# The second layer's product with w1 and w2 in seven half-block products over pairs of 384 tokens

## The chip, the cores and the metric

The kernel runs on one core of a Trainium2 chip. The metric is device time in microseconds (us) from the start to the end of the one launch. TensorE (PE) multiplies, with weight loads (PEld) that overlap; VectorE (DVE), ScalarE (ACT) and GpSimd (POOL) work element by element; SyncE (SP) issues most DMAs. Every engine takes its own instructions in the order in which the kernel wrote them.

## What is computed

Windowed attention over q, k, v (4 batches, 8 heads, 576 positions, 64 wide) gives x of 2304 tokens by 512. Then come two layers, both in float32:

```python
h = x @ w_in                         # 512 -> 2048
x2 = (h * (1.0 / (1.0 + np.exp(-h)))) @ w_out   # 2048 -> 512
a = x2 @ w1                          # 512 -> 1024
b = x2 @ w2                          # 512 -> 1024
out = ((a * b) @ w3) @ w_out2        # 1024 -> 1024 -> 512
```

## The kernel before

A float32 operand is kept as two fp32r parts, high and low (`split`: an ACT copy makes the high part, a DVE subtraction the low one). A product is the sum of three matmuls: high by high, low by high, high by low. The matrices arrive as 64-bit words, a piece being 128 by 512; class `Convert` turns each into its two parts in small steps ("micros"): a load into one of four `raw` buffers, `rebias` (L386, ACT), two `bits` operations (L394 and L396, DVE), `high` (L405, ACT) and `low` (L411, DVE). Letters in the strings `START`, `SLOT` and `GROUP` say where a micro ("m") stands between the parts of the matrix work; so the order of every engine is written by hand.

The first layer runs over five chunks of tokens (`CH1`) and 16 blocks `f` of w_in and w_out: `h_part` (L524), `g_ops`, `g_split`, `x2_part` (L552). Attention is woven into its first chunks. In the last chunk the buffers `wf` of w_in and w_out come free one after the other, and the pieces of w1, w2, w3 and w_out2 are converted into them. x2 is stored to DRAM (`x2d`) chunk by chunk.

The second layer first makes W' = w3 @ w_out2 in two halves (`wp_group`, L503, 96 matmuls each, with the conversion of w3 beside them). Then it runs over five chunks of tokens (`CH2`: four of 512, one of 256) and eight blocks `j` of 128 columns of w1 and w2. For each (chunk, j), `ab_part` (L600) makes a and b, 12 matmuls each: four blocks of the 512 inputs by three products of parts. `p_ops` copies a (L610, ACT) and multiplies by b (L611, DVE); `p_split` splits the product into `pg` (L454, ACT, L455, DVE); `o_part` (L630) multiplies by W' into one PSUM bank for each 128 tokens. a and b have two PSUM banks each. The order is: a and b of the next j, then the output of this j, so that each product has a whole j's time to be split.

## Time and profile before

| what | us |
|---|---|
| median of 3 runs (849.88 to 852.16) | 850.1 |
| the profiled execution | 851.98 |
| its span, first to last instruction | 850.0 |
| PE busy in that span | 829.0 |
| DVE busy | 400.2 |
| ACT busy | 361.1 |
| POOL busy | 56.7 |

The page gives the busy time of each engine, and in 40 slices of 21.25 us where it lies. The chain of waits says which engine's work ended last at each step. The views by line and form give the mean duration of one instruction of each shape; the timeline gives start and duration in order of time, with runs of the same line merged (x12 is twelve instructions); the windows view sums busy time in a stretch.

### The profile page before, as it was taken

The page shows a single profiled execution, that of the slowest core. Times are in us where ns is not written, and L with a number is a line of the kernel's source. Part 1 is how long each engine was busy: PE and PEld are TensorE (multiplying, and loading weights), DVE is VectorE, ACT ScalarE, POOL GpSimd, SP SyncE. Part 2 cuts the span into 40 slices and gives each one's busy share as a digit, 9 for nine tenths or more (in the row PEclk, how much of TensorE's full clock was granted, in tenths as well). Part 3 has the DMA queues.
Part 4 walks back from the last instruction along what each step waited for, and adds up shares of the span by engine and source line. Part 5 has one row for each costly group of instructions (what it writes and reads, how often), then busy time and mean ns, then how long its engine had stood idle before and what let it go on. Part 6 is the DMA issues. An engine that isn't in the chain of part 4 may idle for free.

```text
span 850.0 us, 11943 instructions
## 1 busy us (share of the span) xinstructions
PE 829.0 (98%) x4312; PEld 684.3 (81%) x4312; DVE 400.2 (47%) x1097; ACT 361.1 (42%) x950; POOL 56.7 (7%) x70
## 2 busy tenths in 40 slices
PE   5799999999999999999999999999999999999998
PEld 3467777788788999888888888888888888888897
DVE  4968888455534663222375656683122122112121
ACT  5857777565534763322354543462122122112121
POOL 4311110011100220000000000000000000000000
PEclk9999999999999999999999999999999999999999
DMA  5655555221101311200063326460030030020010
GB/s 166 201 175 180 185 183 172 74 63 50 49 27 41 94 26 49 76 0 1 14 210 124 99 100 222 133 190 1 1 99 1 1 99 1 1 75 0 1 51 26
DMA packets 42635, 69.20 MB, mean 81 GB/s; under 512 B 5328, under 2 KB 25040, under 8 KB 42576
## 3 DMA queue, kind: packets, MB, share of 16 engines
q1 hardware_dynamic: 42208, 68.09, 25.6%
q8 instruction: 34, 0.56, 0.3%
q10 hardware_dynamic: 368, 0.35, 0.2%
q14 instruction: 25, 0.20, 0.1%
HBM read 58.98 MB, written 9.44 MB: 80 GB/s over the span
## 4 chain that ended last, share of the span: by engine, by line
PE 95%; DMA 2%; DVE 2%; SPq 0%; ACT 0%; issue 0%; POOL 0%; POOLq 0%
PE x L552 24%; PE h L524 24%; PE ab L600 23%; PE o L630 12%; PE wp L503 5%; PE o L256 2%; PE s L185 2%; PE s L190 2%; PE t L238 2%; DMA raw_i<-in_w_in_dram 1%; DMA kz<-in_kT_dram 1%; DVE sm L206 1%; DVE at L245 0%; SPq L162 0%; DVE xT L267 0%
## 5 line engine op out<-in xcount | busy, mean ns | idle before, releaser
L552 PE MATMUL x<-g,wf 128*128 128x512 f32 (+1 forms) x960 | 217.7, 371 | 0.0
L524 PE MATMUL h<-xT,wf 128*128 128x512 f32 (+1 forms) x960 | 217.2, 373 | 0.0
L600 PE MATMUL ab<-xT,wf 128*128 128x512 f32 (+1 forms) x960 | 203.7, 368 | 0.0
L600 PEld LDWEIGHTS ab<-xT,wf 128*128 128x128 f32 x960 | 168.2, 188 | 30.6
L524 PEld LDWEIGHTS h<-xT,wf 128*128 128x128 f32 x960 | 167.5, 190 | 29.7
L552 PEld LDWEIGHTS x<-g,wf 128*128 128x128 f32 x960 | 166.2, 188 | 30.9
L611 DVE TENSOR_TENSOR pa<-pa,ab 128x512 f32<-128x512 f32 (+1 forms) x40 | 25.4, 635 | 189.3 <-PE ab L600 188.4
L535 DVE SCALAR_TENSOR_TENSOR t<-t,h 128x512 f32<-128x512 f32 (+1 forms) x80 | 50.6, 632 | 129.2 <-ACT t L534 129.1
L630 PE MATMUL o<-wf,pg 128*128 128x512 f32 x432 | 104.3, 390 | 0.0
L630 PEld LDWEIGHTS o<-wf,pg 128*128 128x128 f32 x432 | 80.6, 188 | 16.4
L534 ACT ACTIVATE t<-h 128x512 f32<-128x512 f32 (+1 forms) x80 | 44.1, 551 | 104.9 <-PE h L524 102.7
L218 ACT ACTIVATE sm<-sm,nm 96x128 f32<-96x128 f32 x192 | 74.5, 390 | 11.3 <-DVE nm L206 11.3
L610 ACT ACTIVATE pa<-ab 128x512 f32<-128x512 f32 (+1 forms) x40 | 22.2, 555 | 119.1 <-PE ab L600 119.1
L230 POOL TENSOR_TENSOR sm<-sm,rs 96x512 f32<-96x512 f32 x48 | 51.9, 1081 | 263.6 <-DVE rs L228 130.0
L455 DVE TENSOR_TENSOR g<-t,g 128x512 fp32r<-128x512 f32 (+1 forms) x80 | 54.4, 680 | 31.8 <-ACT g L454 30.7
L454 ACT ACTIVATE pg<-pa 128x512 fp32r<-128x512 f32 (+1 forms) x40 | 23.6, 589 | 104.2 <-DVE pa L611 104.2
L454 ACT ACTIVATE g<-t 128x512 fp32r<-128x512 f32 (+1 forms) x80 | 46.8, 586 | 30.0 <-DVE t L535 29.7
L206 DVE CUSTOM_DVE_ANT_0 sm<-s,mask 96x128 f32<-96x128 f32 x192 | 43.8, 280 | 8.4 <-POOL ident masks.py:199 4.3
L503 PE MATMUL wp<-wf,xT 128*128 128x512 f32 x192 | 43.9, 389 | 0.0
L503 PEld LDWEIGHTS wp<-wf,xT 128*128 128x128 f32 x192 | 36.0, 188 | 7.5
L190 PE MATMUL s<-kz,q 128*96 128x256 f32 x112 | 31.3, 409 | 7.4 <-DMA kz<-in_kT_dram 7.4
L455 DVE TENSOR_TENSOR pg<-pa,pg 128x512 fp32r<-128x512 f32 (+1 forms) x40 | 25.6, 639 | 26.3 <-ACT pg L454 26.3
(63 smaller groups left out, 595.4 us busy)
## 6 DMA issues: line engine op xcount, KB each, us to landing
raw_i<-in_w_in_dram SPq DMA_DIRECT2D x16, 512.0 KB, 4.3
raw_u<-in_w_out_dram SPq DMA_DIRECT2D x16, 512.0 KB, 5.7
raw<-in_w_dram SPq DMA_DIRECT2D x16, 512.0 KB, 3.3
raw_w<-in_w_dram SPq DMA_DIRECT2D x16, 512.0 KB, 4.4
v<-in_v_dram SPq DMA_DIRECT2D x96, 64.0 KB, 2.5
kz<-in_kT_dram SPq DMA_DIRECT2D x95, 56.0 KB, 2.5
q<-in_qT_dram SPq DMA_DIRECT2D x15, 288.0 KB, 2.9
x2d<-x2s SPq DMA_DIRECT2D x8, 512.0 KB, 3.3
```

The costliest lines, as they stand in the source:

```text
L190: nc.tensor.matmul(s_ps[:QB, c], t[:, QB * i:QB * i + QB], kz[n % 3][:, :, k0:k0 + P], start=True, stop=True,)
L206: nc.vector.tensor_tensor_reduce(sm[:, c, h], s_ps[:QB, c, h], mask[:, mo + c], -SCALE, 3.0e38, ALU.add, ALU.min, nm[:, 2 * c + h:2 * c + ...
L218: nc.scalar.activation(sm[:, c, h], sm[:, c, h], AF.Exp, bias=nm[:, j:j + 1], scale=-1.0, accum_out=su[:, j:j + 1],)
L230: nc.gpsimd.tensor_tensor(f, f, rs.to_broadcast([QB, 4, P]), op=ALU.mult)
L454: nc.scalar.activation(dst[:, 0], src, AF.Copy)
L455: nc.vector.tensor_sub(dst[:, 1], src, f32(dst[:, 0]))
L503: nc.tensor.matmul(wp_ps[i], a[:, i // 2, sa, i % 2 * P:(i % 2 + 1) * P], o[:, sb], start=(jt == 0 and x == 0), stop=(jt == NG - 1 and x = ...
L524: nc.tensor.matmul(ps, win(f, sa, kt), xT[:, kt, sb, r0:r0 + n], start=(kt == 0 and x == 0), stop=(kt == KT - 1 and x == 2),)
L535: nc.vector.scalar_tensor_tensor(t, t, 1.0, ps, op0=ALU.add, op1=ALU.mult)
L552: nc.tensor.matmul(xps[c][m][:, :n], wout(f, sa, m), g[:, sb], start=(f == 0 and sa == 0 and sb == 0), stop=(f == NF - 1 and sb == 1),)
L600: nc.tensor.matmul(ps[:, :n], w12(j, x, sa, kt), xT[:, kt, sb, r:r + n], start=(kt == 0 and y == 0), stop=(kt == KT - 1 and y == 2),)
L630: nc.tensor.matmul(ops[c][m], g[:, sa, m * P:(m + 1) * P], wp_v(j, sb), start=(j == 0 and sa == 0 and sb == 0), stop=(j == NG - 1 and sa = ...
```

## The change

a and b are made by Strassen's scheme in Winograd's form. Weights and x2 are cut in half along the 512 inputs; the 1024 columns of w1 are paired as block j with block j + 4 and those of w2 likewise; tokens are paired as two blocks of 384 (`T2`), so 2304 tokens are three pairs (`NPR`). A "set" is one of w1, w2 with one j of 0 to 3: eight sets. Each set and pair takes seven products (`PROD`) of half blocks, 6 matmuls each (two input blocks by three products of parts) with 384 columns, where the same piece of work had eight such products.

The weight operand of a product is a half block or a sum of half blocks: `Jobs.combine` makes the four sums of a set (on DVE for sets 0 to 2, on POOL for sets 3 to 7), and `high` and `low` split seven units of 256 columns per set instead of the four that the two pieces hold. The token operands are likewise half blocks or sums (`x_sum`, `x_split`), seven per pair. `collect` adds up the seven products from two PSUM banks: the first is copied to s1 by ACT, the others are added by DVE, seven additions per set. When w2's set of a j has been added too, the four blocks of a * b are multiplied (on POOL in the first pair, on DVE in the others), copied by ACT and split by DVE. `o_group` is three matmuls of the output; twelve of them per two sets stand one behind each product.

Four sets fit in SBUF. All eight are stored to DRAM (`set_io`) as they are made, and in the second and third pair four of them are loaded back; the order of the sets turns round in every other pair. The first two sets' products stand between the parts of W''s second half. W''s first half uses the PSUM banks that attention had, and its first group stands inside the last block of the first layer.

```diff
 CH1 = [(0, 512), (512, 512), (1024, 256), (1280, 512), (1792, 512)]
-CH2 = [(0, 512), (512, 512), (1024, 512), (1536, 512), (2048, 256)]
-R2 = [0, 512, 0, 512, 1024]
+T2 = 384
+NPR = NT // (2 * T2)
+NSET = NG
...
-    "hmmHmxXmmtgmm",
+    "hmHmxtgmmmmXmmmm",
 )
-LAST_SLOT = "ahxXHtg"
-GROUP = "mmmmmmmmmmmmmmmwmmmmmmW"
+GROUP = ("mmmmw", "mmmmW")
+MICROS = 2
...
+    setd = [dram.tile([P, 7, 512], F32, tag=f"set{i}", name=f"setd_{i}") for i in range(NSET)]
...
+    def set_io(s, store):
+        for part, n in ((0, 4), (1, 3)):
+            t = f32(wf[2 * (s % 4) + part][:, :512 * n])
+            d = setd[s].rearrange("p u k -> p (u k)")[:, 2048 * part:2048 * part + 512 * n]
+            nc.sync.dma_start(out=d, in_=t) if store else nc.sync.dma_start(out=t, in_=d)
...
+        def combine(self, k, x):
+            a, b = self.yf(k, 0), self.yf(k, 1)
+            if x == 0:
+                self.sum[k] = tmp1.tile([P, 4, 256], F32, tag="ss", name=f"ss_{k}")
+            t = self.sum[k]
+            eng = nc.gpsimd if self.jobs[k][1] > 2 else nc.vector
+            if x == 0:
+                eng.tensor_add(t[:, 0], b[:, :256], b[:, 256:])
+            elif x == 1:
+                eng.tensor_sub(t[:, 1], t[:, 0], a[:, :256])
+            elif x == 2:
+                eng.tensor_sub(t[:, 2], a[:, :256], b[:, :256])
+            else:
+                eng.tensor_sub(t[:, 3], a[:, 256:], t[:, 1])
...
+        def low(self, k, i):
+            dst, y = self.parts(k)[i]
+            nc.vector.tensor_sub(dst[:, 1], y, f32(dst[:, 0]))
+            srcs, d = self.jobs[k]
+            if len(srcs) == 2 and i == 2:
+                set_io(d, True)
...
     def wp_group(k, part):
         half, jt = divmod(k, NG)
         if jt == 0 and part == 0:
-            wp_ps[:] = [ps_x.tile([P, 512], F32, tag="x", name=f"wp_{half}_{i}") for i in range(4)]
+            wp_ps[:] = []
+        if jt == 0:
+            for i in range(2 * part, 2 * part + 2):
+                pool, tag = (ps_x, "x") if half else (ps_h, "h") if part else (ps_a, "a")
+                wp_ps.append(pool.tile([P, 512], F32, tag=tag, name=f"wp_{half}_{i}"))
...
+    PROD = [("11", "11"), ("S2", "T2"), ("12", "21"), ("S3", "T3"), ("S1", "T1"), ("22", "T4"), ("S4", "22")]
...
+    def g_block(j, i, s):
+        b = 4 * (j % 2) + i
+        o = 1024 * (b % 2) + T2 * s
+        return wf[8 + b // 2][:, o:o + T2]
...
+    def order(pr):
+        return [0, 1, 2, 3, 4, 5, 6, 7] if pr % 2 == 0 else [6, 7, 4, 5, 2, 3, 0, 1]
...
+    def product(s, i):
+        if not banks:
+            banks[:] = [ps_h.tile([P, 512], F32, tag="h", name=f"bank{k}") for k in range(2)]
+        b = banks[count[0] % 2][:, :T2]
+        count[0] += 1
+        a, x = PROD[i]
+        n = 0
+        for kt in range(2):
+            for sa, sb in ((0, 0), (1, 0), (0, 1)):
                 nc.tensor.matmul(
-                    ps[:, :n], w12(j, x, sa, kt), xT[:, kt, sb, r:r + n],
-                    start=(kt == 0 and y == 0), stop=(kt == KT - 1 and y == 2),
-                )
-        ab[c, j, x] = ps
-    def p_ops(c, j):
-        n = CH2[c][1]
-        a, b = ab.pop((c, j, 0)), ab.pop((c, j, 1))
-        t = gp.tile([P, 512], F32, tag="t", name=f"pa_{c}_{j}", bufs=1)[:, :n]
-        nc.scalar.activation(t, a[:, :n], AF.Copy)
-        nc.vector.tensor_mul(t, t, b[:, :n])
-        pt[c, j] = t
-    def p_split(c, j):
-        n = CH2[c][1]
-        g = gp.tile([P, 2, 512], F32R, tag="g", name=f"pg_{c}_{j}")[:, :, :n]
-        split(g, pt[c, j])
-        pt[c, j] = g
-    def o_part(c, j):
-        t0, n = CH2[c]
-        nm = n // P
-        if j == 0:
-            ops[c] = [ps_x.tile([P, 512], F32, tag="x", name=f"o_{c}_{m}") for m in range(nm)]
-        g = pt.pop((c, j))
-        todo = [(m, 0, sb) for m in range(nm) for sb in (0, 1)] + [(m, 1, 0) for m in range(nm)]
-        if j == NG - 1:
-            todo.sort(key=lambda z: z[0])
-        for m, sa, sb in todo:
+                    b, a_op(s, a, sa, kt), b_op(x, sb, kt),
+                    start=(n == 0), stop=(n == 5),
+                )
+                n += 1
+        return b
...
+    def collect(pr, s, i, b, j):
+        if not cst:
+            for k in ("s1", "u2", "u3", "c11", "c22", "c21", "c12"):
+                cst[k] = fin.tile([P, T2], F32, tag=k, name=k)
+        c = cst
+        s1, u2, u3 = c["s1"], c["u2"], c["u3"]
+        second = s % 2
+        now = [op for at, op in behind if at <= count[0]]
+        behind[:] = [z for z in behind if z[0] > count[0]]
+        if i == 0:
+            nc.scalar.activation(s1, b, AF.Copy)
+        elif i == 1:
+            nc.vector.tensor_add(u2, s1, b)
+        elif i == 3:
+            nc.vector.tensor_add(u3, u2, b)
+        else:
+            k, u, t = {2: ("c11", s1, s1), 4: ("c22", u3, s1), 5: ("c21", u3, u3), 6: ("c12", u2, u2)}[i]
+            nc.vector.tensor_add(t if second else c[k], u, b)
+            if i == 4:
+                nc.vector.tensor_add(u2, u2, b)
+        for op in now:
+            op()
+        if i in (2, 4, 5, 6):
+            if second:
+                n = ("c11", "c22", "c21", "c12").index(k)
+                hi, lo = (g_block(j, n, x) for x in range(2))
+                (nc.gpsimd if pr == 0 else nc.vector).tensor_mul(c[k], c[k], t)
+                nc.scalar.activation(hi, c[k], AF.Copy)
+                behind.append((
+                    count[0] + (2 if pr == 0 else 1), lambda: nc.vector.tensor_sub(lo, c[k], f32(hi))
+                ))
...
+    def o_group(pr, jj, n, m):
+        j = order(pr)[2 * jj] // 2
+        if pr not in ops:
+            ops[pr] = o_begin()
+        f = j + (n in (1, 2)) * (NG // 2)
+        first_ = jj == 0 and n < 2
+        last = jj == NG // 2 - 1 and n >= 2
+        for x, (sa, sb) in enumerate(((0, 0), (0, 1), (1, 0))):
             nc.tensor.matmul(
-                ops[c][m], g[:, sa, m * P:(m + 1) * P], wp_v(j, sb),
-                start=(j == 0 and sa == 0 and sb == 0), stop=(j == NG - 1 and sa == 1),
+                ops[pr][m], g_block(jj, n, sa)[:, m % 3 * P:(m % 3 + 1) * P], wp_v(f, sb),
+                start=(first_ and x == 0), stop=(last and x == 2),
             )
-        if j == NG - 1:
...
+        def weights(k, part):
+            if part == 0:
+                cv2.allowed = W3[min(k + 1, 2 * NG - 1)] + 1
+                cv2.need(W3[k])
+            for x in GROUP[part]:
+                if x == "m":
+                    cv2.micro()
+                else:
+                    wp_group(k, part)
+                    if todo:
+                        x_split(todo.pop(0))
+        def set_products(pr, k, s, between):
+            for i in range(7):
+                b = product(s, i)
+                collect(pr, s, i, b, k // 2)
+                for op, x in RENEW.get((k - NSET if k >= NSET - 2 else k, i), ()):
+                    if pr > 0 if k == 0 else pr + 1 < NPR:
+                        op(x)
+                between(i)
+            if pr > 0 and k < 4:
+                set_io(order(pr)[k + 4], False)
+            if k % 2:
+                new = [(pr, k // 2, n, m) for n in range(4) for m in ((0, 1, 2) if n in (0, 2) else (3, 4, 5))]
+                if (pr, k) == (NPR - 1, NSET - 1):
+                    new.sort(key=lambda z: z[3])
+                groups.extend(new)
...
+        for k in range(1, NG):
+            for part in range(2):
+                weights(k, part)
+        halves = [(k, part) for k in range(NG, 2 * NG) for part in range(2)]
+        weights(*halves.pop(0))
+        weights(*halves.pop(0))
+        for s in range(2):
+            set_products(0, s, s, lambda i: weights(*halves.pop(0)))
+        def between(pr, k, i):
+            if pr == 0:
+                for _ in range(MICROS):
+                    cv2.micro()
+            if groups and not (k % 2 == 0 and i == 0):
+                o_group(*groups.pop(0))
+        for pr in range(NPR):
+            for k, s in enumerate(order(pr)):
+                if pr == 0 and k < 2:
+                    continue
+                if pr == 0:
+                    cv2.allowed = min(len(cv2.jobs), SET[min(s + 3, NSET - 1)] + 1)
+                    cv2.need(SET[s])
+                if k == NSET - 4 and pr + 1 < NPR:
+                    load_x2(pr + 1)
```

In these order rows `bank0` and `bank1` are the two PSUM banks of products, `wf0` to `wf7` the buffers of weight sets, `wf8` to `wf11` those of the split a * b, `wf12` to `wf15` W'; `s1`, `u2`, `u3` and `c11` to `c12` are the running sums; `ss` the four weight sums, `rawj` a raw piece. First PE in the steady part of the second layer, before:

```order
L630 MATMUL o_1_0_5992<-wf12_105,pg_1_0_5932 128x512 x2
L630 MATMUL o_1_1_5993<-wf12_105,pg_1_0_5932 128x512 x2
L630 MATMUL o_1_2_5994<-wf12_105,pg_1_0_5932 128x512 x2
L630 MATMUL o_1_3_5995<-wf12_105,pg_1_0_5932 128x512 x2
L630 MATMUL o_1_0_5992<-wf12_105,pg_1_0_5932 128x512
L630 MATMUL o_1_1_5993<-wf12_105,pg_1_0_5932 128x512
L630 MATMUL o_1_2_5994<-wf12_105,pg_1_0_5932 128x512
L630 MATMUL o_1_3_5995<-wf12_105,pg_1_0_5932 128x512
L600 MATMUL ab0_1_2_6010<-xT_109,wf2_95 128x512 x12
L600 MATMUL ab1_1_2_6023<-xT_109,wf2_95 128x512 x12
L630 MATMUL o_1_0_5992<-wf12_105,pg_1_1_5989 128x512 x2
L630 MATMUL o_1_1_5993<-wf12_105,pg_1_1_5989 128x512 x2
```

and after, in the first pair, from product 4 of set 3 to the first products of set 4:

```order
L818 MATMUL bank1_5423<-xT_112,wf2_98 128x384 x6
L871 MATMUL o_4_5711<-wf12_108,wf11_107 128x512 x3
L818 MATMUL bank0_5422<-xT_112,wf3_99 128x384 x6
L871 MATMUL o_5_5712<-wf12_108,wf11_107 128x512 x3
L818 MATMUL bank1_5423<-wf1_97,wf2_98 128x384 x2
L818 MATMUL bank1_5423<-wf5_101,wf2_98 128x384
L818 MATMUL bank1_5423<-wf3_99,wf2_98 128x384 x2
L818 MATMUL bank1_5423<-wf7_103,wf2_98 128x384
L818 MATMUL bank0_5422<-xT_112,wf5_101 128x384 x6
L818 MATMUL bank1_5423<-xT_112,wf4_100 128x384 x6
L871 MATMUL o_0_5707<-wf13_109,wf8_104 128x512 x3
L818 MATMUL bank0_5422<-xT_112,wf5_101 128x384 x6
```

The 24 matmuls of a and b have become single products of six, one group of three output matmuls stands between two products, and each product's bank is written again two products later; there is no output group behind the first product of an even set.

ACT at the same place, before (one j: the copy of a, the high part of a * b):

```order
L610 ACTIVATE pa_1_2_6036<-ab0_1_2_6010 128x512
L454 ACTIVATE pg_1_2_6039<-pa_1_2_6036 128x512
L610 ACTIVATE pa_1_3_6082<-ab0_1_3_6056 128x512
L454 ACTIVATE pg_1_3_6085<-pa_1_3_6082 128x512
L454 ACTIVATE xT_109<-x2f_2_0_6008 128x512 x2
L610 ACTIVATE pa_1_4_6130<-ab0_1_4_6104 128x512
```

and after, from the end of set 3 to the start of set 5:

```order
L853 ACTIVATE wf10_106<-c11_5433 128x384
L853 ACTIVATE wf10_106<-c22_5434 128x384
L853 ACTIVATE wf11_107<-c21_5435 128x384
L853 ACTIVATE wf11_107<-c12_5436 128x384
L516 ACTIVATE rawj_30_0_5740<-rawj_30_0_5740 128x512
L516 ACTIVATE rawj_30_1_5756<-rawj_30_1_5756 128x512
L836 ACTIVATE s1_5430<-bank0_5422 128x384
L565 ACTIVATE wf3_99<-y2_29_0_5835 128x2x256
L565 ACTIVATE wf3_99<-y2_29_1_5854 128x256
L565 ACTIVATE wf2_98<-ss_29_5871 128x4x256
L516 ACTIVATE rawj_31_0_5838<-rawj_31_0_5838 128x512
L516 ACTIVATE rawj_31_1_5857<-rawj_31_1_5857 128x512
```

ACT's copy of set 4's first product to s1 stands behind the high part of c12 of the sets before it and behind two rebiases.

POOL had nothing after attention; its last rows before the end were

```order
L230 TENSOR_TENSOR sm_43_3448<-sm_43_3448,rs_43_3500 96x512
L230 TENSOR_TENSOR sm_44_3538<-sm_44_3538,rs_44_3581 96x512
L230 TENSOR_TENSOR sm_45_3632<-sm_45_3632,rs_45_3671 96x512
L230 TENSOR_TENSOR sm_46_3711<-sm_46_3711,rs_46_3763 96x512
L230 TENSOR_TENSOR sm_47_3793<-sm_47_3793,rs_47_3836 96x512
```

and now, around the end of set 3, it has

```order
L852 TENSOR_TENSOR c11_5433<-c11_5433,s1_5430 128x384
L852 TENSOR_TENSOR c22_5434<-c22_5434,s1_5430 128x384
L852 TENSOR_TENSOR c21_5435<-c21_5435,u3_5432 128x384
L541 TENSOR_TENSOR ss_29_5871<-y2_29_1_5854 128x256
L543 TENSOR_TENSOR ss_29_5871<-ss_29_5871,y2_29_0_5835 128x256
L852 TENSOR_TENSOR c12_5436<-c12_5436,u2_5431 128x384
L545 TENSOR_TENSOR ss_29_5871<-y2_29_0_5835,y2_29_1_5854 128x256
L547 TENSOR_TENSOR ss_29_5871<-y2_29_0_5835,ss_29_5871 128x256
```

The multiplication for c12 stands behind two of the four weight sums of set 5, on an engine that had nothing here before. On DVE, which had two instructions per j (L611, L455), the additions from the banks now stand between bits operations and low parts; behind c12's addition come the low parts of c22 and c21.

## Rows read from the trace of the kernel before

**Rows 1.** The page: busy time, share and count of PE; its granted clock in 40 slices.
```profile
PE 829.0 (98%) x4312; PEld 684.3 (81%) x4312; DVE 400.2 (47%) x1097; ACT 361.1 (42%) x950; POOL 56.7 (7%) x70
...
PEclk9999999999999999999999999999999999999999
```

**Rows 2.** The page: the chain that ended last, share of the span by engine.
```profile
PE 95%; DMA 2%; DVE 2%; SPq 0%; ACT 0%; issue 0%; POOL 0%; POOLq 0%
```

**Rows 3.** Windows: length, busy PE PEld DVE ACT POOL (count), clock, DMA, GB/s.
```profile
15.00:20.00 5.00, 2.71 (x17) 1.56 (x16) 2.94 (x17) 3.68 (x18) 2.07 (x2) 0.89 0.54 163
...
45.00:50.00 5.00, 4.58 (x21) 3.67 (x22) 1.11 (x3) 1.01 (x2) 0.92 (x1) 0.66 0.70 210
...
425.30:512.30 87.00, 87.00 (x386) 72.03 (x385) 53.27 (x88) 40.79 (x70) 0.00 (x0) 1.00 0.41 135
512.30:566.70 54.40, 54.40 (x241) 45.02 (x240) 38.36 (x64) 27.18 (x47) 0.00 (x0) 1.00 0.57 180
```

**Rows 4.** Timeline of PE in the second layer: start, length, line, shape, count.
```profile
580.34 5.60 PE L600 MATMUL ab<-xT,wf 128*128 128x512 f32 x24
585.78 2.88 PE L630 MATMUL o<-wf,pg 128*128 128x512 f32 x12
...
818.70 3.04 PE L600 MATMUL ab<-xT,wf 128*128 128x256 f32 x24
821.58 1.55 PE L630 MATMUL o<-wf,pg 128*128 128x512 f32 x6
822.96 3.04 PE L600 MATMUL ab<-xT,wf 128*128 128x256 f32 x24
```

**Rows 5.** Groups by line and form: busy us, mean ns of one, idle before.
```profile
L230 POOL TENSOR_TENSOR sm<-sm,rs 96x512 f32<-96x512 f32 x48 | 51.9, 1081 | 263.6 <-DVE rs L228 130.0 <-ACT xT L266 47.1 <-ACT raw_i L386 44.4
...
L454 ACT ACTIVATE pg<-pa 128x512 fp32r<-128x512 f32 x32 | 20.2, 632 | 91.2 <-DVE pa L611 91.2
L610 ACT ACTIVATE pa<-ab 128x512 f32<-128x512 f32 x32 | 19.1, 598 | 103.9 <-PE ab L600 103.9
...
L396 DVE SCALAR_TENSOR_TENSOR y<-raw,y 128x512 int32<-128x512 int32 x16 | 11.1, 692 | 0.5
...
L386 ACT ACTIVATE raw<-raw 128x512 f32<-128x512 f32 x16 | 10.6, 663 | 2.0 <-DMA raw<-in_w_dram 2.0
...
L394 DVE TENSOR_SCALAR y<-raw 128x512 int32<-128x512 int32 x16 | 6.8, 427 | 0.4
...
L611 DVE TENSOR_TENSOR pa<-pa,ab 128x256 f32<-128x256 f32 x8 | 3.4, 422 | 23.3 <-PE ab L600 23.3
...
L610 ACT ACTIVATE pa<-ab 128x256 f32<-128x256 f32 x8 | 3.1, 384 | 15.2 <-PE ab L600 15.2
```

**Rows 6.** Timeline: the same operation back to back on ACT and on DVE.
```profile
587.31 1.14 ACT L454 ACTIVATE xT<-x2f 128x512 fp32r<-128x512 f32 x2
...
588.05 1.29 DVE L455 TENSOR_TENSOR xT<-x2f,xT 128x512 fp32r<-128x512 f32 x2
...
594.21 0.69 DVE L611 TENSOR_TENSOR pa<-pa,ab 128x512 f32<-128x512 f32 x1 [4.88 <-PE ab L600]
```

**Rows 7.** Timeline: POOL's multiplication and DVE's instructions around it, in attention.
```profile
200.62 0.62 DVE L455 TENSOR_TENSOR kr<-kz,kr 128x448 fp32r<-128x448 f32 x1 [0.24 <-ACT kr L454]
...
206.86 0.36 DVE L267 TENSOR_TENSOR xT<-o,xT 128x192 fp32r<-128x192 f32 x1
207.33 1.10 DVE L455 TENSOR_TENSOR kr<-kz,kr 128x448 fp32r<-128x448 f32 x1
...
206.91 1.04 POOL L230 TENSOR_TENSOR sm<-sm,rs 96x512 f32<-96x512 f32 x1 [6.21 <-ACT xT L266]
...
288.15 2.11 POOL L230 TENSOR_TENSOR sm<-sm,rs 96x512 f32<-96x512 f32 x1 [4.63 <-DVE rs L228]
```

**Rows 8.** DMA issues: count, KB of one, median us from issue to landing.
```profile
raw<-in_w_dram SPq DMA_DIRECT2D x16, 512.0 KB, 3.3
```

**Rows 9.** Timeline: start of the first long run of the first layer.
```profile
46.37 7.28 PE L524 MATMUL h<-xT,wf 128*128 128x512 f32 x24
```

## Prediction before the run

> **What bounds the kernel now.** I read the page's busy shares first: PE is busy 829.0 of 850.0 us, at the full clock of 2.4 GHz in every slice [rows 1]. Then the chain of waits: 95% of what ended last is PE [rows 2]. Then windows by stage: in the last chunk of the first layer (425 to 512 us) and in W' with its a and b (512 to 567 us) PE is busy in every microsecond, DVE 53.3 of 87.0 and 38.4 of 54.4 [rows 3]. Last the timeline of PE [rows 4]: 24 matmuls of 512 columns start at 580.34 and the next group at 585.78, so one takes 5.44 / 24 = 0.2267 us; the merged lines hide no gap. So the second layer is a bare sum of matmuls, and any matmul time saved is won unless PE starts to wait.
>
> **Fewer columns on PE.** Before, a and b take 768 matmuls of 512 columns and 192 of 256. The 256 have a price of their own in the last chunk: from 818.70 to 821.58 are 24 of them, 2.88 / 24 = 0.120; the whole period to 822.96 holds 24 and six of 512, (4.26 - 6 x 0.2267) / 24 = 0.1208 [rows 4]. That is 768 x 0.2267 + 192 x 0.1208 = 197.3 us. After, it is 8 sets x 3 pairs x 7 products x 6 = 1008 matmuls of 384 columns, a size that the trace lacks. From below: in proportion to 512, 0.170. From above: on the straight line between the two sizes, (0.2267 + 0.1208) / 2 = 0.1737, the fixed part being some 0.015. I take the line, since 384 lies between its points and the 256 show that a weight load hides behind even a shorter matmul. 1008 x 0.1737 = 175.1: **22.2 us won** (25.9 by the lower price). Output (432 matmuls) and W' (192) keep their number and width, the first layer too.
>
> The 48 matmuls more bring 48 weight loads more. [Rows 4] show 0.1208 for a matmul of 256 columns with its load, so next to nothing of a load stands on the path. The Trainium skill, TensorE: Matmul & The Clock Gate, Part 3 (The mechanism), says that a weight load overlaps a running matmul only where the row groups differ, which they never do here; with that page's 1/1.2 ns per loaded column a load would be 0.107, a 256 would take 0.21, and by an estimate from it the gain would be 17.9 instead of 22.2. The measurement decides against it.
>
> **What the other engines get.** Durations by form [rows 5], 384 columns taken half way between 512 and 256: a DVE addition from PSUM (0.69 [rows 6] + 0.42) / 2 = 0.555, an ACT copy (0.598 + 0.384) / 2 = 0.49, with an fp32r output some 0.03 more. Back to back each costs less: two DVE instructions of 512 take 1.29, two of ACT 1.14 [rows 6], so 0.60 and 0.52 each, the tail of one lying under the next; DVE 0.47 at 384, ACT 0.42. POOL has one row, 1.04 us for 512 columns [rows 7]; by proportion 0.78 for 384 and 0.52 for 256. With all of the 1.04 fixed, both would be 1.04, my upper bound; I take the proportion, because DVE and ACT show little that is fixed.
>
> Per two sets PE has 84 products' matmuls and 36 of the output, 84 x 0.1737 + 36 x 0.2267 = 22.8 us. DVE has, in the first pair, 14 additions and 4 low parts (18 x 0.47 = 8.5), and for two new sets four times both bits operations (0.427 and 0.692 [rows 5] less the overlap: 0.34 + 0.60) and twice the low parts of 512, 256 and 1024 columns (0.60 + 0.34 + 1.14): 7.9. Together 16.4 of 22.8, so DVE keeps up on average. In pairs two and three it has 22 instructions, 10.3 us. The last chunk's DVE work rises (12 weight sums, wider low parts, four token sums and two low parts) to some 66 us by durations against 87.0 of PE; that hides behind PE as 53.3 did, and if a raw piece comes late ACT's rebias blocks the tanh behind it.
>
> **DMA.** Each set is 7 x 512 x 128 floats, 1.84 MB, stored once; twice four sets are loaded back. A 0.52 MB piece lands 3.3 us after its issue [rows 8]; at that rate a set takes 12 us. The loads are issued right behind the set that they overwrite and are needed three sets (34 us) later; four sets in 46 us are 7.3 MB, 160 GB/s, below the 180 that the W' stage moved [rows 3]. I cost DMA at nothing; if a load were late, PE would wait for it once per set.
>
> **Where PE must wait.** Products have two banks. Behind product i, PE does an output group (0.68), product i+1 (1.04) and another group (0.68); then it needs the bank back, 2.4 us after the product's end. At an even set's start one group is missing and the bank is freed by ACT's copy to s1, and this copy stands behind c12 of the sets before. Walk it from the end of product 6 of set 3, at 0: DVE adds c12 at 0.2 to 0.7, its earlier rows being done. POOL must multiply, but the c21 product and two weight sums stand ahead of c12 on its queue, and here counts what the trace shows of POOL beside DVE: a DVE subtraction of two SBUF tensors that takes 0.62 alone takes 1.10 when POOL's 1.04 us began just ahead of it, ending 0.48 behind POOL's end, and POOL took 2.11 amid such subtractions, while a DVE row with a PSUM operand kept 0.36 beside the same POOL row [rows 7]. So the two exclude each other on rows with two SBUF inputs. The two low parts of DVE (0.47 each) and POOL's sums (0.52 each) thus alternate: POOL reaches c12 at 2.9 and ends at 3.7. ACT's high part 0.42, two rebiases (0.663 [rows 5] less the overlap, 0.57 each) and s1 0.49 follow: 5.8. PE is ready for product 2 of set 4 at 0.68 + 1.04 + 1.04 + 0.68 = 3.44: it waits **2.35**. At set 6 no rebias stands there: **1.2**. At pair two no weight sum and no rebias: s1 comes in time, 0. At set 2, right behind W', two high parts of W' and two rebiases stand ahead of c12 on ACT, and DVE's low parts of W' wait for them ahead of the c12 addition: bank 1 comes 1.5 late, and then s1, behind two more high parts of W', another 1.5: **3.0**. In pairs two and three DVE does the multiplication with no lock; s1 ends 2.6 after product 6, PE needs it at 3.44: 0.
>
> W' itself: its first half now carries the token splits too. Walking micros and splits through ACT and DVE from the first layer's end, the fourth group's piece waits for a raw piece that is issued only when a buffer is read (2.6) and lands at 6.5 [rows 8]; the group's third matmul waits until 9.4 and would stand at 8.6: **0.8**. Elsewhere in this half the margin is half a us or more.
>
> **Sum.** Waits: 2.35 + 1.2 + 3.0 + 0.8 = 7.35. I add 1.5 for what a walk by hand misses (a late raw piece, the sets 5 and 7): 8.9. Against the profiled execution: its span 850.0 - 22.2 + 8.9 = 836.7, and 838.7 with the 1.98 around the span. The median of the runs is 1.9 below the profiled 851.98, so as a median **837**. The end is alike (a copy from PSUM and a store) and costs nothing either way. With waits from 4 to 14 the time is 832 to 842: the forecast's own range.
>
> **Rivals.** *The waits are covered.* If POOL wins the lock each time or its rows are shorter, c12 is early and two banks suffice: waits of 0 to 4 at either price of a matmul, 824 to 832, about 829. For it: DVE is at 72% on average. Against it: the place of s1 on ACT's queue, which no average moves. Chance 0.18.
>
> *The clock falls at the waits.* In the start of the kernel PE idles between small groups, and the granted clock is 0.89 in 15 to 20 us and 0.66 in 45 to 50 [rows 3], where part of the time ran at 1.2 GHz instead of 2.4; the 24 matmuls that started in the latter took 7.28 instead of 5.60 [rows 4, 9], 1.7 more. Four waits at 1.7: +7, 844 (842 to 848). Against it: work is dense on both sides of each wait here, and sparse there. The Trainium skill, TensorE: Matmul & The Clock Gate, section Why this matters for your kernels, says to avoid idle gaps between bursts of matmuls, since they throttle the clock; the early slices agree, for 2 to 3 us between dense work no run here shows it. Chance 0.12.
>
> *POOL's queue paces the first pair: slower.* If each of POOL's four rows around an even set's start takes the 2.11 of the contended row [rows 7], c12 ends near 8.2 rather than 3.7, and each boundary costs some 6 us or more; beside sets 2, 4, 6 and pair two the odd sets' sums, too, come late and the new sets with them. The change loses from the point where the waits pass 22.2 + 2.6 = 25 us: four boundaries of 7 are 28, 856. For it: the row exists and DVE is busy three quarters of this time. Against: the mean of POOL's 48 rows is 1.08 [rows 5], so few were so long. Chance 0.10.
>
> *No change.* Waits of 20 to 25 in many places (late pieces in the last chunk, new sets late): 847.5 to 852.6, chance 0.07. Below 824: 0.03.
>
> **How the numbers follow.** The forecast has 0.50. From 827 to 848 lie it, most of the first rival and the clock's case, some 0.8. Measurement tells 0.3% (2.6 us) from no change. Faster: 0.50 + 0.18 + 0.12 + 0.03 = 0.83; same 0.07; slower 0.10.
>
> **What would show it.** A mean of about 0.174 us per product matmul from start to start; PE idle at the start of sets 2, 4 and 6, released by ACT's s1 or by DVE, and none at a set's start in pairs two and three; POOL's rows near 0.78 and 0.52, longer beside DVE. Wrong would be: waits of PE on DMA, a granted clock below 0.95 behind W', idle PE in the last chunk of the first layer, or waits spread over every product, which would mean that two banks are too few.

## Result and profile after: the change made the kernel slower

The changed kernel takes 859.24 us (median of 4 runs, 858.46 to 863.36), the kernel before 849.99 in the same session: ratio 1.0113, 95% interval 1.0077 to 1.0150. The forecast was 837 (827 to 848): the time moved the other way. The profiled execution took 858.46 us, span 855.3.

The page of the changed kernel, busy time, clock, chain, and the groups (busy us, mean ns | idle us before, released by):

```profile
PE 822.1 (96%) x4360; PEld 693.9 (81%) x4360; DVE 510.0 (60%) x1301; ACT 361.5 (42%) x954; POOL 89.3 (10%) x106
...
PEclk9999999999999999999999999999999999999999
...
PE 87%; DVE 5%; ACT 2%; POOL 2%; DMA 2%; issue 2%; SPq 0%; POOLq 0%; DVEq 0%; ACTq 0%
...
L818 PE MATMUL bank<-xT,wf 128*128 128x384 f32 x864 | 177.6, 342 | 10.7 <-ACT s L836 5.0
...
L852 POOL TENSOR_TENSOR c<-c,s 128x384 f32<-128x384 f32 x8 | 9.0, 1121 | 273.6 <-DVE s L843 273.6
```

Against [rows 1, 2] PE is busy 6.9 us less, where some 22 were forecast, and in the chain PE has lost 8 points to engines that it waits for. What PE waits for behind the first layer (510 us on):

```profile
PE bank L818 <- ACT s L836: 5.0, 3, 3.0
PE bank L818 <- DVE u L843: 4.9, 4, 2.6
PE bank L818 <- DVE u L845: 1.4, 2, 1.2
PE wp L653 <- ACT wf L565: 1.0, 1, 1.0
PE bank L818 <- ACT xT L776: 0.5, 2, 0.3
```

The columns are total us, times, longest. Together with two shorter lines these are 13 us of waits, where [rows 4] had none. The timeline of PE in steady work of pair two, start and length:

```profile
700.20 1.22 PE L818 MATMUL bank<-wf,wf 128*128 128x384 f32 x6
701.26 2.24 PE L818 MATMUL bank<-xT,wf 128*128 128x384 f32 x12
703.34 0.86 PE L871 MATMUL o<-wf,wf 128*128 128x512 f32 x3
704.04 1.23 PE L818 MATMUL bank<-xT,wf 128*128 128x384 f32 x6
705.11 0.86 PE L871 MATMUL o<-wf,wf 128*128 128x512 f32 x3
705.81 1.22 PE L818 MATMUL bank<-xT,wf 128*128 128x384 f32 x6
```

A product takes 1.07 from start to start and a group 0.70, one period 1.77 us, though nothing waits. The sum had 6 x 0.1737 + 3 x 0.2267 = 1.72. Where no group stands between, the trace has the forecast's pace: of the 18 matmuls in a row from 700.20 the last 12 take 703.34 - 701.26 = 2.08 us, 0.173 each. Inside an interleaved product the six steps are 169, 177, 185, 176, 182, 173 ns, in a group 229, 233, 236, the same all the way: a matmul right behind a change of width is slower, and with a change every 6 and every 3 matmuls the pace never settles.

At the start of set 4 (PE, POOL, ACT, DVE, from their timelines):

```profile
594.95 1.23 PE L818 MATMUL bank<-wf,wf 128*128 128x384 f32 x6
597.18 2.35 PE L818 MATMUL bank<-xT,wf 128*128 128x384 f32 x12 [1.01 <-DVE u L843]
599.37 0.86 PE L871 MATMUL o<-wf,wf 128*128 128x512 f32 x3
603.19 2.29 PE L818 MATMUL bank<-xT,wf 128*128 128x384 f32 x6 [2.96 <-ACT s L836]
605.28 1.28 PE L871 MATMUL o<-wf,wf 128*128 128x512 f32 x3
```
```profile
598.08 1.05 POOL L541 TENSOR_TENSOR ss<-y 128x256 f32<-128x256 f32 x1
599.22 0.95 POOL L543 TENSOR_TENSOR ss<-ss,y 128x256 f32<-128x256 f32 x1
600.12 0.99 POOL L852 TENSOR_TENSOR c<-c,u 128x384 f32<-128x384 f32 x1
```
```profile
601.15 0.52 ACT L853 ACTIVATE wf<-c 128x384 fp32r<-128x384 f32 x1 [2.46 <-POOL c L852]
601.58 1.19 ACT L516 ACTIVATE rawj<-rawj 128x512 f32<-128x512 f32 x2
602.67 0.47 ACT L836 ACTIVATE s<-bank 128x384 f32<-128x384 f32 x1
```
```profile
594.38 1.12 DVE L856 TENSOR_TENSOR wf<-c,wf 128x384 fp32r<-128x384 f32 x1
595.43 0.42 DVE L521 TENSOR_SCALAR y<-rawj 128x512 int32<-128x512 int32 x1
595.88 0.69 DVE L526 SCALAR_TENSOR_TENSOR y<-rawj,y 128x512 int32<-128x512 int32 x1
596.49 1.01 DVE L843 TENSOR_TENSOR u<-u,bank 128x384 f32<-128x384 f32 x2
```

It is the chain of the forecast: c12's multiply behind two sums on POOL, its high half on ACT, two rebiases, then s1. It took longer than walked: s1 ends 7.0 us behind the end of product 6 (603.14 against 596.18), not 5.8. DVE was late already (a low part of 1.12 us beside a POOL row, then bits), which gives PE a wait of its own, 1.01, that the forecast lacks; the three POOL rows are 0.95 to 1.05. Behind the longer wait PE ran at half speed: the product at 603.19 takes 2.09 from start to start instead of 1.06. The windows say the same (length, busy PE PEld DVE ACT POOL, clock, DMA, GB/s):

```profile
600.00:603.00 3.00, 0.23 (x1) 0.00 (x0) 0.00 (x0) 1.85 (x4) 2.48 (x4) 0.96 1.04 397
603.00:606.40 3.40, 3.21 (x10) 2.98 (x10) 2.51 (x6) 3.05 (x6) 0.00 (x0) 0.53 0.58 204
```

At the start of set 2 (POOL, ACT, DVE, PE):

```profile
567.25 1.02 POOL L852 TENSOR_TENSOR c<-c,u 128x384 f32<-128x384 f32 x1
568.30 0.52 ACT L853 ACTIVATE wf<-c 128x384 fp32r<-128x384 f32 x1 [3.56 <-POOL c L852]
570.43 1.29 DVE L459 TENSOR_TENSOR wf<-wp,wf 128x512 fp32r<-128x512 f32 x2 [4.30 <-ACT wf L458]
572.24 2.29 PE L818 MATMUL bank<-xT,wf 128*128 128x384 f32 x6 [2.57 <-DVE u L843]
```

c21's multiply, which also stands behind two sums on POOL, holds ACT; behind it ACT does two rebiases and the high parts of W', for which DVE's low parts wait, ahead of c12's addition. The forecast's walk has the rebiases and the high parts there, but not POOL.

**The account.** From the starts of PE's matmuls, for the profiled executions, with 173.5 and 226.7 ns as the settled pace; each line is what the trace has beyond the forecast's term:

| | forecast | trace | difference |
|---|---|---|---|
| changes of width: products 2.9, groups 2.4, W' 0.5 | 0 | 5.8 | +5.8 |
| waits: W' 1.9, set 2 2.7, set 4 4.4, set 6 3.4, pair two 3.1, pair three 2.2, end 0.2 | 8.9 | 17.9 | +9.0 |
| half clock behind the waits of sets 2 and 4 | 0 | 3.0 | +3.0 |
| x2 in the first layer, first matmul to the layer's end (456.1 before, 459.9 after) | 0 | 3.8 | +3.8 |
| first x2 matmul starts at 50.75 instead of 53.48 | 0 | -2.7 | -2.7 |

Waits are counted here from start to start, with the slower first matmuls behind each, so they come to more than the 13 us of idle in the list. Together +18.9, less 0.2 for the products' pace; the span is 855.3 where 836.7 was forecast, +18.6. The last line is a chance of the execution, not of the change: in the runs below the first x2 matmul starts anywhere from 51.2 to 54.4.

### The profile page after: what moved, and what is told of

It reads as the page before. It is cut to its first block, busy times and chain, and to the rows that moved or that the text cites. A ratio compares the mean times of both kernels' runs of the same rounds, so it can differ in the third digit from the quotient of the medians.

```text
span 855.3 us, 12379 instructions
## 1 busy us (share of the span) xinstructions
PE 822.1 (96%) x4360; PEld 693.9 (81%) x4360; DVE 510.0 (60%) x1301; ACT 361.5 (42%) x954; POOL 89.3 (10%) x106
## 2 busy tenths in 40 slices
DMA packets 47789, 98.58 MB, mean 115 GB/s; under 512 B 5872, under 2 KB 28144, under 8 KB 45680
## 4 chain that ended last, share of the span: by engine, by line
PE 87%; DVE 5%; ACT 2%; POOL 2%; DMA 2%; issue 2%; SPq 0%; POOLq 0%; DVEq 0%; ACTq 0%
PE x L702 24%; PE h L674 23%; PE bank L818 18%; PE o L871 10%; PE wp L653 4%; PE s L195 2%; PE o L261 2%; PE s L190 2%; PE t L243 2%; ACT xT L776 1%; POOL c L852 1%; DMA kz<-in_kT_dram 1%; DVE wf L856 1%; DVE s L843 1%; DVE sm L211 1%
## 5 line engine op out<-in xcount | busy, mean ns | idle before, releaser
L818 PE MATMUL bank<-xT,wf 128*128 128x384 f32 x864 | 177.6, 342 | 10.7 <-ACT s L836 5.0
L818 PEld LDWEIGHTS bank<-xT,wf 128*128 128x128 f32 x864 | 154.9, 190 | 27.7 <-ACT s L836 8.4
L871 PE MATMUL o<-wf,wf 128*128 128x512 f32 x432 | 123.0, 397 | 0.0
L871 PEld LDWEIGHTS o<-wf,wf 128*128 128x128 f32 x432 | 79.9, 189 | 7.3 <-DVE wf L856 0.4
L853 ACT ACTIVATE wf<-c 128x384 fp32r<-128x384 f32 x48 | 25.2, 525 | 119.5 <-DVE c L852 73.9
L459 DVE TENSOR_TENSOR g<-t,g 128x512 fp32r<-128x512 f32 (+1 forms) x80 | 54.4, 680 | 31.4 <-ACT g L458 31.3
L836 ACT ACTIVATE s<-bank 128x384 f32<-128x384 f32 x24 | 11.6, 483 | 106.9 <-PE bank L818 106.9
L653 PE MATMUL wp<-wf,wf 128*128 128x512 f32 x192 | 47.2, 393 | 1.3 <-ACT wf L565 1.0
L653 PEld LDWEIGHTS wp<-wf,wf 128*128 128x128 f32 x192 | 35.6, 188 | 8.8 <-ACT wf L565 1.4
L852 POOL TENSOR_TENSOR c<-c,s 128x384 f32<-128x384 f32 x8 | 9.0, 1121 | 273.6 <-DVE s L843 273.6
L272 DVE TENSOR_TENSOR xT<-o,xT 128x192 fp32r<-128x192 f32 (+6 forms) x58 | 18.4, 318 | 30.4 <-ACT xT L271 29.7
```

Source lines behind the costliest of these rows:

```text
L459: nc.vector.tensor_sub(dst[:, 1], src, f32(dst[:, 0]))
L653: nc.tensor.matmul(wp_ps[i], a[:, i // 2, sa, i % 2 * P:(i % 2 + 1) * P], o[:, sb], start=(jt == 0 and x == 0), stop=(jt == NG - 1 and x = ...
L818: nc.tensor.matmul(b, a_op(s, a, sa, kt), b_op(x, sb, kt), start=(n == 0), stop=(n == 5),)
L871: nc.tensor.matmul(ops[pr][m], g_block(jj, n, sa)[:, m % 3 * P:(m % 3 + 1) * P], wp_v(f, sb), start=(first_ and x == 0), stop=(last and x ...
```

## Experiments

Theory A: three separate causes, the queues of the first pair, the changes of width, and the place of g. The rivals stand with each run. Times are medians against before in the same session (849.99 to 850.91).

**The order on ACT (e1).** c12's high half behind the copy to s1:

```diff
-                nc.scalar.activation(hi, c[k], AF.Copy)
+                high = lambda: nc.scalar.activation(hi, c[k], AF.Copy)
+                if pr == 0 and i == 6:
+                    behind.append((count[0] + 1, high))
+                else:
+                    high()
```


> In the first pair of token blocks ScalarE rounds c12's high half only after it has copied the next set's first product (s1); nothing else changes. Theory A (the waits at the starts of sets 4 and 6 are ScalarE's order: s1 stands behind a high half that waits for the POOL multiply, itself behind two POOL sums): the waits of 2.96 and 1.87 us on s1 go, and so does the stretch at half clock behind the first of them (1.4 us): about 6 us less, 853. Rival B (POOL and VectorE between them are too slow for the pace of these sets, whichever engine is asked first): the waits come back on other adds, under 2 us less, 857 or more.

852.99 us, ratio 1.0035 (1.0019 to 1.0052). All PE waits on ACT's s1 are gone from the list, and so is the slow stretch of set 4; one wait of 0.8 on DVE (L840) is new. That ACT's order made the waits on s1 is shown; DVE's (4.9 and 1.4) stay.

**The work on POOL (e2, e9).** e2 puts sums and multiplies on DVE (both cuts); e9 only the multiplies (the second cut):

```diff
-            eng = nc.gpsimd if self.jobs[k][1] > 2 else nc.vector
+            eng = nc.vector
...
-                (nc.gpsimd if pr == 0 else nc.vector).tensor_mul(c[k], c[k], t)
+                nc.vector.tensor_mul(c[k], c[k], t)
```


> The sums of sets 3 to 7 and the multiplies of the first pair go from POOL to VectorE. Theory A (the slow POOL rows of about 1.0 us, and the VectorE rows that run beside them at up to twice their time, make the waits): VectorE's own rows go back to 0.55 and 1.1 us, c12's high half is 2 to 3 us earlier, the s1 waits of 2.96 and 1.87 us shrink to under 1 us: 3 to 6 us less, 853 to 856. Rival B (VectorE itself is full in the first pair): 4 sums of 0.45 and, every second set, 4 multiplies of 0.55 us, 5.8 us per two sets, stretch the first pair by up to that much each: 862 to 874.

> Only the multiplies of the first pair go from POOL to VectorE; the sums of sets 3 to 7 stay on POOL. Theory A (what counts is that c12's multiply stands behind two sums of about 1 us in POOL's queue): both s1 waits go, as in the no-POOL run, 850.5 to 852. Rival B (what counts is that VectorE's rows run at up to twice their time beside any POOL row): half of the no-POOL run's gain of 8 us stays out, 854 to 857.

e2: 851.23 us, ratio 1.0007 (0.9998 to 1.0017), under the 853 to 856 of its theory A. e9: 850.14 us, ratio 0.9989 (0.9978 to 1.0000). So the 16 multiplies of the first pair on POOL, 17.6 us of rows there, cost 9.1 us between the medians (10.5 by the ratios), the half-clock stretches among them: behind W' e2 and e9 have none while PE works. The waits of e9:

```profile
PE bank L818 <- ACT s L836: 2.8, 3, 1.5
PE bank L818 <- DVE u L843: 2.4, 3, 1.0
```

The time is that of theory A, but not all of its waits went: those on s1 fell from 5.0 to 2.8 us, the longest to 1.5, at set 4. POOL's sums still run beside DVE at 0.73 to 0.86 us on average, and rows of DVE beside them still take 1.09 instead of 0.55, c12's multiply of set 3 among them. Yet e9 is not slower than e2, where POOL does nothing here. So in this kernel the lock alone is cheap; the price comes from a POOL row that ACT, and behind ACT PE, is waiting for. Rival B of e2 (DVE full) falls: with all of it on DVE the kernel is 8 us faster than the changed one, not slower.

**The changes of width (e3, e5).** e3 issues two groups after every second product:

```diff
-            if groups and not (k % 2 == 0 and i == 0):
-                o_group(*groups.pop(0))
+            if i % 2:
+                for _ in range(min(2, len(groups))):
+                    o_group(*groups.pop(0))
```


> From set 2 on the output groups are issued two after every second product instead of one after each; the same matmuls. Theory A (a change of width between a 384-column product and a 512-column group costs TensorE some 0.04 us in the matmuls behind it, whatever they read): half as many changes, so half of the 5.3 us that products and groups take above 173.5 and 226.7 ns a matmul: 2.7 us less, 856.5, if the waits stay. Rival B (each of these matmuls is slow by where its operands lie): products still 177 and groups still 233 ns on average, no change within 0.3%.

854.95 us, ratio 1.0045 (1.0030 to 1.0060); 856.5 was expected. Its steady timeline:

```profile
704.77 2.25 PE L818 MATMUL bank<-xT,wf 128*128 128x384 f32 x12
706.86 1.55 PE L871 MATMUL o<-wf,wf 128*128 128x512 f32 x6
708.24 2.25 PE L818 MATMUL bank<-xT,wf 128*128 128x384 f32 x12
```

Twelve and six take 3.47 us where the changed kernel needs 2 x 1.76. Over the second layer the surplus falls from 5.3 to 2.5 us, 2.8 less (2.7 was expected); in the profiled executions waits give 0.8 more, and a later start takes 1.9 back. The same operands at the same places run faster with fewer changes, so rival B falls: what is saved was not in the operands. e5 is the kernel before with the width alone, six blocks of 384 tokens:

```diff
-CH2 = [(0, 512), (512, 512), (1024, 512), (1536, 512), (2048, 256)]
-R2 = [0, 512, 0, 512, 1024]
+CH2 = [(384 * i, 384) for i in range(6)]
+R2 = [0, 384, 768, 0, 384, 768]
```


> The kernel before, with six blocks of 384 tokens in the second layer instead of four of 512 and one of 256; no scheme, no stored operands. Theory A (the width alone costs what the steady rows say): 1152 matmuls at 173.5 ns instead of 768 at 226.7 and 192 at 119.7 is 2.8 us more, and 48 changes between 24 products and 9 output matmuls at 0.04 us are 1.9 us more: 854.5 with the output's 432 matmuls unchanged. Rival B (the changes of width cost nothing by themselves, and what was seen comes from the operands of the scheme): 852 to 853, and the 9 output matmuls of a slot at 226.7 ns throughout.

856.86 us, ratio 1.0074 (1.0055 to 1.0093). Its steady timeline:

```profile
702.66 2.24 PE L630 MATMUL o<-wf,pg 128*128 128x512 f32 x9
704.74 4.35 PE L600 MATMUL ab<-xT,wf 128*128 128x384 f32 x24
708.93 2.24 PE L630 MATMUL o<-wf,pg 128*128 128x512 f32 x9
```

From start to start a and b take 200.9 us instead of 197.1 and the output 99.6 instead of 97.9: 2.8 is the steady price of 1152 matmuls at 173.5 ns, 2.7 the 48 pairs of changes (1.9 was expected). The 9 output matmuls take 2.08 us here, 231 ns each, not 226.7; in the kernel before, a, b and output alternate as well, but mostly at one width, and their sums lie within 0.3 us of the steady price. So it is the width and not the alternation, and rival B falls again. Thus 384 tokens at a time cost 5.5 us of matmuls before any scheme is there to repay it.

**The place of g (e4, e10, e11).** The start address of the first layer's g tiles in a partition is moved, in e4 by moving a small pool from ahead of them, which shifts neighbouring pools too; the other operand of the x2 matmuls stays:

```diff
-    stp = ctx.enter_context(tc.tile_pool(name="stp", bufs=4))
...
+    stp = attn.enter_context(tc.tile_pool(name="stp", bufs=4, side="right"))
```


> The pool of the first layer's g tiles is placed 384 bytes lower in each partition, so that its tiles start at 1664 instead of 0 bytes above a multiple of 2048 (before the change: 640; the weights and xT: 1152); nothing else changes in the program's order. Theory A (the x2 matmuls grew from 227 to 234 ns in the middle by where g lies): x2 falls from 220.8 to about 217.7 us busy and the first layer ends 1 to 3 us earlier: 856 to 858. Rival B (they wait for something else that the change moved): x2 stays at 220 to 221 us, no change.

e10 and e11 leave that pool where it is and put a tile of 128 or 256 bytes ahead of g:

> The first layer's g tiles lie 128 bytes higher than in the changed kernel (128 above a multiple of 2048; weights and xT 1152 above one). Theory A (what matters is that the distance between g and the weights is a multiple of 512 bytes, as it is before the change and where g was moved by 384 bytes): x2 busy 217.7 us, from its first to its last matmul 456 us instead of 459.7. Rival B (a multiple of 512 above a 1024 boundary, or something of the pool's place itself): 220 us or more, 459 to 460.

> The first layer's g tiles lie 256 bytes higher than in the changed kernel: distance to the weights 896 bytes above a multiple of 1024. Theory A (a multiple of 512 is needed): x2 busy 220 us or more, first to last matmul 459 to 460. Rival B (any place but the one at 0 will do): 217.7 and 456.

The groups of x2's 512-column matmuls, of the kernel before, the changed one, e4, e10 and e11 (g at 640, 0, 1664, 128, 256 above a multiple of 2048):

```profile
L552 PE MATMUL x<-g,wf 128*128 128x512 f32 x768 | 191.3, 392 | 0.0
```
```profile
L702 PE MATMUL x<-g,wf 128*128 128x512 f32 x768 | 194.5, 396 | 0.0
```
```profile
L702 PE MATMUL x<-g,wf 128*128 128x512 f32 x768 | 191.4, 392 | 0.0
```
```profile
L704 PE MATMUL x<-g,wf 128*128 128x512 f32 x768 | 191.3, 392 | 0.0
```
```profile
L704 PE MATMUL x<-g,wf 128*128 128x512 f32 x768 | 194.5, 396 | 0.0
```

From the first x2 matmul to the end of the layer they take 459.9, 456.2, 456.3 and 459.9 us; before (g at 640) 456.1. Fast are the three whose distance to the weights (at 1152) is a multiple of 512 bytes, slow the two whose distance is not. The five places do not tell 512 from 256, nor the distance from the place itself (the fast ones all lie 128 above a multiple of 512); why it is so no run here shows. e4's median, 858.78 us (ratio 1.0083, 1.0054 to 1.0112), above the 856 to 858 of its theory A, hides the gain, since its runs met more half-speed stretches behind the same waits: spans go from 852.6 us at a mean granted clock of 0.994 to 859.1 at 0.984. At equal clock it is faster: 852.6 against the changed kernel's 855.3 at 0.994, 854.2 against 856.9 at 0.992. Of e10 and e11 one time each is at hand (856.94, 859.55); only the pace is read from them.

**The sets' traffic (e6).** Stores and loads left out:

```diff
-            nc.sync.dma_start(out=d, in_=t) if store else nc.sync.dma_start(out=t, in_=d)
+            pass
```


> The changed kernel without the stores of the operand sets and without their loads in the second and third pair, which then multiply whatever lies in the buffers: that part of the computation is left out. Theory A (the traffic hides): nothing waits less, 858 to 860. Rival B (stores and loads of about 22 MB slow the engines that share the memory, or loads come late): 3 us less or more, and products or VectorE rows shorter in the second pair.

861.00 us, ratio 1.0126 (1.0093 to 1.0159), with 69.22 instead of 98.58 MB moved and nearly the same list of waits (14.0 us instead of 13.4). The 29.4 MB (the expectation said 22) cost nothing that the end shows.

**Together (e7, e8, e12).** e1, e2, e3 and e4 in one, and the rounding of the second half of W' moved behind the next product's add:

```diff
-                split(quarter(12 + j // 2, j % 2), wp_ps[i])
+                do = lambda j=j, p=wp_ps[i]: split(quarter(12 + j // 2, j % 2), p)
+                if half:
+                    behind.append((count[0] + 1, do))
+                else:
+                    do()
```


> Put together: c12's high half after s1 (the late-high run), sums and multiplies on VectorE (the no-POOL run), output groups two and two, g moved, and the second half of W' rounded after the next product's add instead of before it. If the parts add up: 859.2 less 6 to 8 for the waits and the clock behind them, 2.8 for the changes of width, 3.7 for x2, 1 for W': 844 to 846. If VectorE, full in the first pair, takes the gains back: 848 to 851.

841.84 us, ratio 0.9902 (0.9885 to 0.9918): the parts add up to more than expected, 2 us under the range of 844 to 846; where these 2 us come from was not taken apart. e8 moves groups and preparation steps as well:

> As the combined run, with the output groups after products 1, 4 and 6 of a first set and 2, 4 and 6 of a second, and the preparation of later sets issued where VectorE has fewest adds (2, 3, 2, 2, 3, 2, 2 steps behind the products of a first set, 3, 3, 3, 2, 1, 0, 2 of a second). If the waits left at the set starts come from VectorE's order: 1 to 3 us under the combined run, 842 to 844. If VectorE is simply full there: the same within 1 us.

843.21 us, ratio 0.9918 (0.9903 to 0.9933), a miss: with groups behind three or two products by turns new waits of 0.4 to 0.6 us stand in pairs two and three. e12 keeps two and two and takes only the steps:

```diff
-                for _ in range(MICROS):
+                for _ in range(((2, 3, 2, 2, 3, 2, 2), (3, 3, 3, 2, 1, 0, 2))[k % 2][i]):
```


> The combined run with the preparation of later sets issued in the uneven steps of the spread run (2, 3, 2, 2, 3, 2, 2 behind the products of a first set, 3, 3, 3, 2, 1, 0, 2 of a second). If the pairs of waits of 0.9 and 0.7 us at the starts of sets 4 and 6 are VectorE's preparation ahead of the adds that free the banks: they fall to one of 0.8 us each, 840 to 841. If VectorE is full there whatever the order: 841.5 to 842.5.

840.63 us (838.43 to 841.02), ratio 0.9879 (0.9863 to 0.9896): 1.2% faster than before. Against e7 (0.9885 to 0.9918) the intervals overlap; that the steps gain is seen in PE's idle time behind the first layer, 4.0 us instead of 6.6, not in the time. The first line of its page:

```profile
PE 812.0 (97%) x4360; PEld 690.4 (83%) x4360; DVE 517.7 (62%) x1337; ACT 361.2 (43%) x954; POOL 57.1 (7%) x70
```

and its longest waits of PE behind the first layer:

```profile
PE bank L822 <- DVE u L842: 1.8, 3, 1.1
PE wp L653 <- ACT wf L565: 0.7, 1, 0.7
PE bank L822 <- ACT xT L780: 0.6, 1, 0.6
```

The 10.7 us of idle before the products of the changed kernel's page line are 3.0, no stretch of matmuls behind W' is at half clock, and the runs of e7 lie within 0.6 us, those of the changed kernel within 5.

## Why the prediction was wrong, point by point

By the account above, the sum failed in four places: the waits (8.9 forecast, 17.9 found), the changes of width (nothing forecast, 5.8 found), x2 in the first layer (nothing, 3.8) and the half clock (nothing in the sum, 3.0). The 22 us that fewer columns save were there.

- **The products' price: right, with a term missing.** The line between 512 and 256 gave 0.1737 us; settled runs have 0.1735. That a change of width slows the matmuls behind it was not in the sum: 5.8 us, of which e3 wins back 2.8 with half the changes. [Rows 4] held the sign of it: the six 512-column matmuls between 256-column ones take 822.96 - 821.58 = 1.38 us instead of 6 x 0.2267 = 1.36, and the change makes some 130 such groups out of 8.
- **"The first layer keeps its matmuls": wrong by 3.8 us.** Number and width stay, but the new order of pools moves g, and x2 pays. The diff's pool lines were read for space, not for addresses.
- **The waits at sets 2, 4 and 6: right in place, too short.** Set 4: 2.35 against 4.4, set 6: 1.2 against 3.4, through the chain that was walked; in W' 0.8 against 1.9. The failed step is POOL "by proportion": 0.78 and 0.52 became 1.08 to 1.12 and 0.73 to 0.86 on average. Eleven of the 16 multiplies took 0.99 to 1.02, close under the upper bound of 1.04, the other five 1.12 to 1.66. The second is "its earlier rows being done" for DVE: its add for c12 ended 1.3 us behind product 6's end (597.50 against 596.18), not 0.7, because a low part ran into POOL's row and two bits operations stand behind it. Set 2, 3.0 forecast and 2.7 found, came near by luck: two waits of 1.5 were walked, on DVE and on s1; there was one, of 2.57 us of idle, on DVE, with POOL's multiply for c21 at its head. With the multiplies on DVE (e9) the two waits are there, 1.03 and 0.83.
- **"Pair two 0, pairs two and three no wait": wrong.** 3.1 and 2.2 us. The longest of pair two (1.18, on DVE's add at L845) goes with POOL's multiplies in e2 and e9, so it is the first pair's tail; ones of 0.2 to 0.6 us stay in the other runs. The walk followed c12's chain alone there and left out the token splits, though some of these waits are on them (ACT xT L776).
- **The rival of the clock: right, but not instead of the forecast.** It came on top: 1.6 and 1.4 us behind two waits, close to its 1.7 each, and the clock below 0.95 behind W' that the forecast named as a sign of being wrong is there (0.53). The Trainium skill, TensorE: Matmul & The Clock Gate, section Why this matters for your kernels, advises against idle gaps between bursts of matmuls; the trace agrees behind these two waits of 2.6 and 3.0 us, though they are no longer than the gaps it warns of. The same wait did not always cost this: in e6 full clock followed 2.98 us of idle (the product takes 1.17 from start to start), in e4 half clock followed 1.89 (1.66), and what decides between them no run here shows:

```profile
606.98 1.33 PE L818 MATMUL bank<-xT,wf 128*128 128x384 f32 x6 [2.98 <-ACT s L836]
608.15 0.86 PE L871 MATMUL o<-wf,wf 128*128 128x512 f32 x3
```
```profile
633.46 1.86 PE L818 MATMUL bank<-xT,wf 128*128 128x384 f32 x6 [1.89 <-ACT s L836]
635.12 1.48 PE L871 MATMUL o<-wf,wf 128*128 128x512 f32 x3
```

- **POOL's queue (856, chance 0.10): the nearest to the time,** though its mechanism was not quite this: no row took 2.11 us (the longest 1.66), and odd sets were not late. Without the multiplies on POOL the time is back at 850.
- **DMA at nothing, the lock of DVE and POOL, weight loads hidden:** borne out (e6, the 1.12 us row, the settled 0.1735).
- **The range:** it took waits from 4 to 14 for the worst of the forecast's own case, with the other terms exact. Three omitted costs of 3 to 6 us, each below one percent, all had the same sign. The scheme does gain once the causes are removed: e12's span is 836.2, where 836.7 was forecast. That the two are so close is luck: e12 still pays for changes of width, waits less than the forecast's 8.9, and its first x2 matmul starts 2.3 us earlier than before (51.15 against 53.48).

## What to carry to other kernels

A scheme that trades matmuls for adds moves its cost to queues: for each place where PE reuses a bank, walk back through every engine's order, and be slow to put on POOL a row that an engine ahead of PE waits for (9 us here). Keep matmuls of one width together, and count the changes as a price. When a change rearranges memory pools, compare the addresses of the operands of work that was not to change.

## What the runs showed of the hardware

- Between 384- and 512-column matmuls a change of width costs: one product of six and one group of three take 1062 + 698 ns when they alternate, 1040 + 680 when they do not (+40 ns a pair); with 24 and 9 matmuls, some 56 ns a pair.
- x2's matmuls of 512 columns start mostly 227 ns apart with g at 640, 1664 or 128 bytes above a multiple of 2048 and the weights at 1152, mostly 229 and 238 ns with g at 0 or 256: 3.7 us over this layer.
- On POOL a multiplication of two 128x384 tiles took 1.08 to 1.12 us on average (0.99 to 1.66), an addition of 128x256 0.73 to 0.86; DVE has 0.55 and 0.42 (e2). A DVE row of 128x384 with two SBUF inputs took up to 1.19 beside POOL's rows instead of 0.55, one with a PSUM input 0.54 to 0.56.
- Behind idle of 2.6 and 3.0 us PE ran for some 3 us at 1.2 GHz in the profiled execution (a granted clock of 0.53 over 603.0 to 606.4 us), and other executions of the same kernel lost more (mean clock 0.994 to 0.986, spans 855.3 to 861.6 us). In e6 full clock followed idle of 2.98 us, in e4 half clock idle of 1.89.
